# Two quarters of a weight matrix loaded in blocks of 32 partitions

## The chip, the cores and the metric

The kernel runs on one core of one Trainium2 chip. The metric is the device time of one execution in microseconds (us), lower is better. A time of a kernel is the median of several executions. The profile is of one further execution, and its own time is given beside its span, which runs from the first to the last instruction.

## The reference

The computation is a chunked state-space scan over a sequence (4 batches, 8 heads, 768 positions, head width 32, state width 16), followed by a two-layer feed-forward block with a tanh-gelu. Cut to what matters:

```python
for c in range(nc):                       # chunks of the sequence
    cum = np.cumsum(log_a[:, :, sl], axis=-1)
    L = np.exp(cum[..., :, None] - cum[..., None, :]) * causal
    M = np.einsum('bhin,bhjn->bhij', Cc, Bc) * L
    y_intra = np.einsum('bhij,bhjd->bhid', M, xc)
    y_inter = np.einsum('bhin,bhnd->bhid', Cc, state) * np.exp(cum)[..., None]
    y[:, :, sl] = y_intra + y_inter
    state = decay_full * state + sum_j(Bc * xc * decay_from_j)
x = y.transpose(0, 2, 1, 3).reshape(3072, 256)
h = x @ w_in                              # 256 x 2048
g = 0.5 * h * (1 + tanh(c * (h + 0.044715 * h**3)))
out = g @ w_out                           # 2048 x 256
```

`w_in` is 256 x 2048 and `w_out` 2048 x 256, both float32 in memory (2 MB each). The kernel multiplies in bfloat16.

## The kernel before

The 3072 tokens are cut into 24 chunks of 128 (six for each batch), and two neighbouring chunks make a unit `u` of 256 tokens, 12 units in all. A unit passes through two halves. In the scan half TensorE computes `G` (products of C and B), VectorE masks them (`M`), TensorE forms `Y` into the tile yb, and `yev` copies yb into `xm`, the input of the feed-forward half. There `s1.u.i` (eight steps, i = 0 to 7) multiplies `xm` by 256 columns of `w_in` into an accumulator hp, `gelu.u.i` evaluates it into gT on ScalarE, and `s2.u.k.q` multiplies gT by `w_out`; `oev` copies the result out of the accumulator and `store` writes it to memory.

The weights come in quarters. `load_wi(q)` brings 512 columns of `w_in` into a tile `wf` of 128 partitions x 2 x 512 float32: partition d holds the columns of row d and of row 128 + d. Each is 512 KB. `load_wo(q)` brings a quarter of `w_out` into another such tile. `f_wi(q, k, eng)` and `f_wo` (steps `wi.q.k` and `wo.q.k`) then cast one half of such a tile to bfloat16, into `w_in_sb` or `w_out_sb`, each on the engine that the order names. Steps `s1.u.0` and `s1.u.1` use quarter 0 of `w_in`, `s1.u.2` and `s1.u.3` quarter 1, and so on: `s1.0.0` needs `wi.0.0` and `wi.0.1`, `s1.0.2` needs `wi.1.0` and `wi.1.1`, `s1.0.4` quarter 2, `s1.0.6` quarter 3. `s2.0.0.0` needs both halves of `wo.0`.

The order of all steps is written out by hand in the string `ORDERED`: steps are issued in this order, and each engine runs its own ones in that sequence. A suffix names the engine (`:A` ScalarE, `:D` VectorE, `:P` GpSimd, `:S` SyncE's queue), and `~9` stands for small matmuls on zeros (tile wz) that fill time on TensorE. Nearly all loads are issued by SyncE, one after the other: first the inputs of the first batch (`load_bc0`, `load_aq`, `load_x4`, `load_a`), then the weights mixed with later inputs. In the stretch around the change the order of the loads on SyncE is `load_x4`, `load_a.1`, `load_wi.0`, `load_wi.1`, `load_wi.2`, `load_wo.0`, `load_wi.3`, `load_bc1.0`, `load_wo.1`, `load_bc1.1`, `load_wo.2`, `load_wo.3`, and then the inputs of the second batch.

Every load completes on one of eight counters, which the rows of the order call DMAHW0 to DMAHW7. They are taken in rotation over the loads of SyncE and ScalarE together, in the order of the program. A load therefore waits until the load eight places ahead of it has landed, and an instruction that reads a loaded tile waits on the counter of that load. Within the names of the profile, `wf<-in_moe_w_in_dram` is `load_wi`, `x_t<-in_x_dram` of 512 KB is `load_x4`, `a_t<-in_a_dram` is `load_a`, and `bcf` is `load_bc0` and `load_bc1`.

Of the kernel before, what the change touches and what calls it, by code (L numbers as in the profile page):

```python
# [13 lines left out]

XL = 6
WFB = 8

SCR = (2, 3)
ORDERED = """
# [68 lines left out]
def kernel(  # L88
# [10 lines left out]
    nc = tc.nc  # L99
# [21 lines left out]
    ld = ctx.enter_context(tc.tile_pool(name="ld", bufs=2))  # L121
    wfp = ctx.enter_context(tc.tile_pool(name="wfp", bufs=WFB))
    ldx = ctx.enter_context(tc.tile_pool(name="ldx", bufs=XL))
# [21 lines left out]
    XF, X16, WF = {}, {}, {}  # L145
# [39 lines left out]
    wi = moe_w_in.rearrange("(k d) f -> d k f", d=128)  # L185
    wo = moe_w_out.rearrange("(q p k) m -> q p k m", p=128, k=4)

    def load_wi(q):
        WF[("i", q)] = wfp.tile([128, 2, 512], FP32, name="wf")
        nc.sync.dma_start(out=WF[("i", q)], in_=wi[:, :, q * 512:(q + 1) * 512])  # L190

    def load_wo(q):
        WF[("o", q)] = wfp.tile([128, 4, d_model], FP32, name="wf")
# [565 lines left out]
    bl = {(b, i): add("S", load_bc, b, i) for b in range(1, batch) for i in (1, 0)}  # L759
    xl = {u: add("S", load_x, u) for u in range(2, NU)}  # L760
    wl = {(k, q): add("S", f, q) for k, f in (("i", load_wi), ("o", load_wo)) for q in range(4)}

    win = {(q, k): add("P", f_wi, q, k, alt="PAD", deps=[wl[("i", q)]]) for q in range(4) for k in range(2)}
# [86 lines left out]
    for u in range(NU):  # L850
# [23 lines left out]
        for c in cs:  # L874
            if c % CPB == CPB - 1:
                continue
            p, p1 = (None if c % CPB == 0 else pdq if c < R4 else pd), pdq if c < R4 - 1 else pd
# [22 lines left out]
    for u in range(NU):  # L900
        for i in range(NI):
            q = (2 * i + 1) // 4
# [19 lines left out]

    pools = {"hp": 2, "o": 1, "ga": 1, "gb": 1, "yb": 1, "wf": WFB, "xl": XL, "ld": 2, "ob": 6, "st": 4, "sp": 4}
    for w in ORDERED.split():
        if w[0] == "~":
            fill(yb, int(w[1:]))
        else:
            w, _, n = w.partition("+")
# [34 lines left out]
```

## Time and profile before

| | |
|---|---|
| median of 3 executions | 116.68 us (116.48 to 117.45) |
| the profiled execution | 117.7 us, span 116.0 us |
| granted TensorE clock | 1.00 |
| TensorE matmul busy | 110.1 us, 95% of the span |
| VectorE / ScalarE / GpSimd busy | 70.9 / 73.7 / 17.1 us |
| moved by DMA | 15.97 MB, mean 138 GB/s |
| loads of `w_in` | 4 of 512 KB, median 8.0 us from issue to landing |
| loads of `w_out` | 4 of 512 KB, median 8.6 us from issue to landing |

In the rows of the profile PE is TensorE's matmuls, PEld its weight loads, DVE VectorE, ACT ScalarE, POOL GpSimd, SP SyncE, and SPq the DMA queue that SyncE issues to. L316, for instance, is line 316 of the kernel. The line of a copy is that of a helper (`copy`: L314 on ScalarE, L316 on GpSimd, L318 on VectorE), so copies are told apart by the tiles they write. A row of the timeline gives the start in us, the duration, the engine and line, what is written from what, a count, and in brackets the idle time of the engine ahead of it with what ended it. A row on a load (the listing of issues) gives the count, the size and the median time from the start of the issue to the landing.

### The profile page before, as it was taken

Reading aid. Unit: us, or ns where it says so; the run is one execution under the profiler, and the core shown is the slowest. Engines: PE = TensorE matmul, PEld = TensorE weight load, DVE = VectorE, ACT = ScalarE, POOL = GpSimd, SP = SyncE. Lnnn points to the kernel's source line nnn. Section 1 sums busy time; section 2 is a strip of 40 time slices with the busy share of each in tenths; the row PEclk is TensorE's granted clock in tenths of the full one; section 3 lists DMA queues with packets and bytes.
Section 4 is the critical chain, followed back from the end, with each engine's and each line's share of the span. In section 5 each row is a group of like instructions: output and inputs, shape, how many; then the busy total and the mean of one; then the engine's idle time right before and its main releaser. Section 6 shows DMA issues by size and latency. Waiting matters only on the chain.

```text
span 116.0 us, 3378 instructions
## 1 busy us (share of the span) xinstructions
PE 110.1 (95%) x1427; PEld 91.9 (79%) x1427; DVE 70.9 (61%) x139; ACT 73.7 (64%) x142; POOL 17.1 (15%) x35
## 2 busy tenths in 40 slices
PE   6969989999999999999999999999999999999990
PEld 2335568988788897998989889979979898999970
DVE  6589999789979995664967729221968326100000
ACT  3109679996469774766674567776767766776510
POOL 6552556622220220002000000000000000000000
DMA  3999997979979705999869893000014003200222
GB/s 71 235 242 249 403 325 197 359 138 210 221 122 206 156 4 165 178 199 255 164 174 177 206 90 104 0 0 6 0 51 139 0 6 107 74 0 6 90 96 85
DMA packets 43006, 15.97 MB, mean 138 GB/s; under 512 B 36656, under 2 KB 41456, under 8 KB 42992
## 3 DMA queue, kind: packets, MB, share of 16 engines
q1 hardware_dynamic: 42848, 15.68, 57.8%
q8 instruction: 11, 0.18, 0.6%
q10 hardware_dynamic: 144, 0.08, 0.3%
q14 instruction: 3, 0.02, 0.1%
HBM read 11.04 MB, written 3.93 MB: 129 GB/s over the span
## 4 chain that ended last, share of the span: by engine, by line
PE 88%; DVE 2%; ACT 2%; issue 0%
PE hp L709 37%; PE o_ps L727 34%; PE ga L595 3%; PE yb L727 3%; PE yb L659 3%; PE yb L650 3%; PE yb L697 2%; PE hp L628 1%; DVE cz L409 1%; PE hp L425 1%; ACT gT L713 1%; ACT xm L314 1%; DVE pe L387 1%; PE o_ps L563 0%; PE ga L484 0%; DVE s_new L676 0%
## 5 line engine op out<-in xcount | busy, mean ns | idle before, releaser
L713 ACT ACTIVATE gT<-hp 128x512 bf16<-128x512 f32 x96 | 53.9, 596 | 22.0 <-PE hp L709 21.4
L709 PE MATMUL hp<-xm,w_in_sb 128*128 128x256 bf16 x384 | 52.4, 273 | 0.7 <-ACT x L314 0.6
L727 PE MATMUL o_ps<-w_out_sb,gT 128*128 128x256 bf16 x352 | 47.5, 273 | 0.0
L709 PEld LDWEIGHTS <-w_in_sb 128*128 128x128 bf16 x384 | 41.4, 114 | 4.0 <-issue 3.2
L727 PEld LDWEIGHTS <-gT 128*128 128x128 bf16 x384 | 37.0, 98 | 4.2 <-issue 0.2
L605 DVE TENSOR_TENSOR m<-ga,tri 128x1024 bf16<-128x1024 f32 x12 | 14.6, 1216 | 0.3 <-PE gb L595 0.3
L318 DVE COPY o_sb<-o_ps 128x256 f32<-128x256 f32 x13 | 5.5, 423 | 14.6 <-PE o_ps L727 10.9
L605 DVE TENSOR_TENSOR m<-gb,tri 128x1024 bf16<-128x1024 f32 x11 | 13.4, 1214 | 0.0
L697 PE MATMUL yb<-wz 128*128 128x512 bf16 (+3 forms) x26 | 8.1, 459 | 1.1 <-DVE warm L222 1.1
L683 DVE SCALAR_TENSOR_TENSOR sp_new<-s_new,pend,bmask 128x256 bf16<-128x256 f32 x17 | 8.3, 503 | 0.1
L314 ACT ACTIVATE xm<-yb 128x512 bf16<-128x512 f32 x10 | 6.0, 598 | 2.7 <-PE yb L659 2.0
L316 POOL CAST x<-x_t 128x512 bf16<-128x512 f32 x6 | 3.7, 613 | 24.5 <-PE hp L709 9.9
L697 PEld LDWEIGHTS <-wz 128*128 128x128 bf16 x27 | 3.0, 121 | 5.0 <-issue 3.2
L314 ACT ACTIVATE o_sb<-o_ps 128x256 f32<-128x256 f32 x9 | 3.3, 384 | 4.5 <-PE o_ps L727 4.1
L659 PE MATMUL yb<-m,x 128*32 128x128 bf16 x192 | 6.2, 220 | 0.0
L676 DVE SCALAR_TENSOR_TENSOR s_new<-s_new,pend,hp 128x64 f32<-128x64 f32 x13 | 3.6, 279 | 4.1 <-PE hp L628 3.9
L650 PE MATMUL yb<-ce,sp_new 128*32 128x128 bf16 x160 | 5.3, 221 | 0.0
L674 DVE COPY s_new<-hp 128x64 f32<-128x64 f32 x3 | 0.7, 225 | 6.8 <-PE hp L628 6.8
L595 PE MATMUL ga<-ce,bh 32*128 32x256 bf16 x48 | 4.7, 272 | 0.0
L595 PE MATMUL gb<-ce,bh 32*128 32x256 bf16 x48 | 4.7, 273 | 0.0
L316 POOL CAST w_out_sb<-wf 128x512 bf16<-128x512 f32 x6 | 3.9, 672 | 3.7 <-DMA wf<-in_moe_w_out_dram 3.7
L659 PEld LDWEIGHTS <-x 128*32 128x32 bf16 x192 | 3.8, 97 | 0.7 <-issue 0.4
(109 smaller groups left out, 79.6 us busy)
## 6 DMA issues: line engine op xcount, KB each, us to landing
out_dram<-o_sb SPq DMA_DIRECT2D x24, 128.0 KB, 1.8
x_t<-in_x_dram SPq DMA_DIRECT2D x20, 128.0 KB, 3.8
wf<-in_moe_w_in_dram SPq DMA_DIRECT2D x4, 512.0 KB, 8.0
wf<-in_moe_w_out_dram SPq DMA_DIRECT2D x4, 512.0 KB, 8.6
bc_t<-in_B_dram SPq DMA_DIRECT2D x3, 384.0 KB, 4.3
bc_t<-in_C_dram SPq DMA_DIRECT2D x3, 384.0 KB, 4.3
scr<-bc SPq DMA_DIRECT2D x4, 192.0 KB, 2.0
x_t<-in_x_dram SPq DMA_DIRECT2D x1, 512.0 KB, 5.3
```

Of the source, the lines that this page charges most:

```text
L314: nc.scalar.activation(o, i, AF.Copy)
L316: nc.gpsimd.tensor_copy(out=o, in_=i)
L318: nc.vector.tensor_copy(out=o, in_=i)
L595: nc.tensor.matmul(out=gbank(g)[:, 256 * k:256 * k + 256], lhsT=bh_of(2 * u + k)[gs], rhs=ce_of(2 * u + k)[gs], start=True, stop=True, til ...
L605: nc.vector.tensor_tensor(out=m_of(u)[:, 2 * i:2 * i + 2].rearrange("p g k e t -> p (g k e) t"), in0=gx[i].rearrange("p g (k t) -> p (g k) ...
L650: nc.tensor.matmul(out=y4[32 * j:32 * j + 32, k, w], lhsT=sp[:, 32 * h:32 * h + 32], rhs=ce_of(gc)[:, h % 2], start=first(j), stop=False, ...
L659: nc.tensor.matmul(out=y4[32 * j:32 * j + 32, k, w], lhsT=X16[u][:, k, 32 * h:32 * h + 32], rhs=m[:, h // 2, h % 2, :], start=first(j), st ...
L683: nc.vector.scalar_tensor_tensor(out=sp_new.rearrange("p (g d) -> p g d", g=4), in0=(XN[0][:, H * D:H * D + 64] if gc == 0 else state[("s" ...
L697: nc.tensor.matmul(out=t[:, 0:m * 128], lhsT=wz, rhs=w3.to_broadcast([128, m, 128]), start=True, stop=True, skip_group_check=True)
L709: nc.tensor.matmul(out=hp[:, j * T:(j + 1) * T], lhsT=w_in_k[:, w, q, k], rhs=xm[:, w, u * T:(u + 1) * T], start=(w == 0), stop=(w == 1))
L713: nc.scalar.activation(gts[u][:, 2 * i:2 * i + 2], hps.pop((u, i)).rearrange("p (j t) -> p j t", j=2), AF.Gelu_apprx_tanh)
L727: nc.tensor.matmul(out=ops[gc], lhsT=gts[u][:, fi, k * Q:(k + 1) * Q], rhs=w_out_sb[:, fi, :], start=(fi == 0 and (u > 0 or k == 0)), stop ...
```

## The change

`load_wi(0)` and `load_wi(1)` are each issued as four transfers, one for every block of 32 partitions of the tile; `load_wi(2)` and `load_wi(3)` stay one transfer each. The bytes, their places and the order of all steps are the same.

```diff
+WI_PARTS = (4, 4, 1, 1)
...
     def load_wi(q):
         WF[("i", q)] = wfp.tile([128, 2, 512], FP32, name="wf")
-        nc.sync.dma_start(out=WF[("i", q)], in_=wi[:, :, q * 512:(q + 1) * 512])
+        n = 128 // WI_PARTS[q]
+        for p in range(0, 128, n):
+            nc.sync.dma_start(out=WF[("i", q)][p:p + n], in_=wi[p:p + n, :, q * 512:(q + 1) * 512])
```

On SyncE's queue this stands before the change from `load_a.1` to `load_bc1.1`; wf_204, wf_251, wf_258 and wf_433 are the four quarters of `w_in`, and each row ends with the counter that it waits on, the one it will itself complete on:

```order
L162 DMA a_t_99<-in_a_dram 32x384 [waits DMAHW0_49]
L190 DMA wf_204<-in_moe_w_in_dram 128x2x512 [waits DMAHW1_49]
L190 DMA wf_251<-in_moe_w_in_dram 128x2x512 [waits DMAHW2_49]
L190 DMA wf_258<-in_moe_w_in_dram 128x2x512 [waits DMAHW3_49]
L194 DMA wf_303<-in_moe_w_out_dram 128x1024 [waits DMAHW4_49]
L190 DMA wf_433<-in_moe_w_in_dram 128x2x512 [waits DMAHW5_49]
L155 DMA bcf1_101<-in_B_dram 128x8x32 [waits DMAHW6_49]
L194 DMA wf_449<-in_moe_w_out_dram 128x1024 [waits DMAHW7_49]
L155 DMA bcf1_101<-in_C_dram 128x8x32 [waits DMAHW0_49]
```

After the change the same stretch up to `load_bc1.0` reads as follows; lines below the function are three higher, and wf_254, wf_264 and wf_439 are now quarters 1, 2 and 3:

```order
L193 DMA wf_204<-in_moe_w_in_dram 32x2x512 [waits DMAHW1_49]
L193 DMA wf_204<-in_moe_w_in_dram 32x2x512 [waits DMAHW2_49]
L193 DMA wf_204<-in_moe_w_in_dram 32x2x512 [waits DMAHW3_49]
L193 DMA wf_204<-in_moe_w_in_dram 32x2x512 [waits DMAHW4_49]
L193 DMA wf_254<-in_moe_w_in_dram 32x2x512 [waits DMAHW5_49]
L193 DMA wf_254<-in_moe_w_in_dram 32x2x512 [waits DMAHW6_49]
L193 DMA wf_254<-in_moe_w_in_dram 32x2x512 [waits DMAHW7_49]
L193 DMA wf_254<-in_moe_w_in_dram 32x2x512 [waits DMAHW0_49]
L193 DMA wf_264<-in_moe_w_in_dram 128x2x512 [waits DMAHW1_49]
L197 DMA wf_309<-in_moe_w_out_dram 128x1024 [waits DMAHW2_49]
L193 DMA wf_439<-in_moe_w_in_dram 128x2x512 [waits DMAHW3_49]
L156 DMA bcf1_101<-in_B_dram 128x8x32 [waits DMAHW4_49]
```

SyncE issues six transfers more. Quarter 2 used to wait for the load of aq eight places ahead, and now waits for the first part of quarter 0; the loads behind it up to `load_wo.3` wait for parts of quarters 0 and 1 in turn.

GpSimd casts a half of each of the first three quarters; before the change (wf is the quarter's tile, 0, 1 and 2 in this order):

```order
L316 CAST w_in_sb_141<-wf_204 128x512 [waits DMAHW1_49]
L316 CAST w_in_sb_141<-wf_251 128x512 [waits DMAHW2_49]
L316 CAST w_in_sb_141<-wf_258 128x512 [waits DMAHW3_49]
L316 CAST w_in_sb_141<-wf_258 128x512
L316 CAST w_out_sb_142<-wf_303 128x512 [waits DMAHW4_49]
```

And after it:

```order
L319 CAST w_in_sb_141<-wf_204 128x512 [waits DMAHW3_49,DMAHW4_49,DMAHW2_49,DMAHW1_49]
L319 CAST w_in_sb_141<-wf_254 128x512 [waits DMAHW6_49,DMAHW7_49,DMAHW5_49,DMAHW0_49]
L319 CAST w_in_sb_141<-wf_264 128x512 [waits DMAHW1_49]
L319 CAST w_in_sb_141<-wf_264 128x512
L319 CAST w_out_sb_142<-wf_309 128x512 [waits DMAHW2_49]
```

The sequence of the casts is the same. Each cast of quarters 0 and 1 now waits for four counters in place of one, and so do the casts of the same quarters on ScalarE (`wi.0.0`) and VectorE (`wi.1.0`).

## The prediction

> **What bounds the kernel now.** I read the page first. Of the chain that ended last it says:
>
> ```profile
> PE 88%; DVE 2%; ACT 2%; issue 0%
> ```
>
> So the kernel stands on TensorE. Next I cut the span into stages and asked for TensorE alone (columns: stage, its length, TensorE's busy time with its count of matmuls, granted clock, DMA share, GB/s):
>
> ```profile
> 0.00:13.70 13.70, 11.58 (x161) 1.00 0.84 230
> 13.70:16.00 2.30, 1.68 (x16) 1.00 1.12 359
> 16.00:20.00 4.00, 3.90 (x59) 1.00 0.85 230
> 20.00:112.00 92.00, 92.00 (x1195) 1.00 0.54 116
> 112.00:116.00 4.00, 0.93 (x9) 1.00 0.29 98
> ```
>
> From 20 to 112 us TensorE has no idle time at all. The total is thus 92 us plus the drain of 4 us plus whatever it takes to get to the point where TensorE runs through. Only the first 20 us can give or take anything, and there the table of waits lists what TensorE waited for (total, times, longest):
>
> ```profile
> PE yb L697 <- DVE warm L222: 1.1, 1, 1.1
> PE hp L356 <- DVE peq L351: 0.7, 1, 0.7
> PE hp L709 <- ACT x L314: 0.6, 1, 0.6
> PE hp L425 <- DVE cz L409: 0.4, 1, 0.4
> ```
>
> No row names a load, and none names a cast of a weight. The quarters of `w_in` must be on time, but nothing on TensorE waits for them.
>
> **How the loads stand.** SyncE's own timeline shows when each load was issued and how long its issue held SyncE:
>
> ```profile
> 2.86 0.58 SPq L183 DMA_DIRECT2D x_t<-in_x_dram  x1
> 3.49 1.96 SPq L162 DMA_DIRECT2D a_t<-in_a_dram  x1
> 5.50 0.43 SPq L190 DMA_DIRECT2D wf<-in_moe_w_in_dram  x1
> 5.97 0.47 SPq L190 DMA_DIRECT2D wf<-in_moe_w_in_dram  x1
> 6.48 0.47 SPq L190 DMA_DIRECT2D wf<-in_moe_w_in_dram  x1
> 6.99 0.50 SPq L194 DMA_DIRECT2D wf<-in_moe_w_out_dram  x1
> 7.54 0.77 SPq L190 DMA_DIRECT2D wf<-in_moe_w_in_dram  x1
> ...
> 9.07 5.12 SPq L194 DMA_DIRECT2D wf<-in_moe_w_out_dram  x1
> ```
>
> The listing of issues, asked for each of the first seven by itself in the same order, gives the time from the start of the issue to the landing:
>
> ```profile
> x_t<-in_x_dram SPq DMA_DIRECT2D x1, 512.0 KB, 5.3
> a_t<-in_a_dram SPq DMA_DIRECT2D x1, 48.0 KB, 5.2
> wf<-in_moe_w_in_dram SPq DMA_DIRECT2D x1, 512.0 KB, 5.6
> wf<-in_moe_w_in_dram SPq DMA_DIRECT2D x1, 512.0 KB, 7.6
> wf<-in_moe_w_in_dram SPq DMA_DIRECT2D x1, 512.0 KB, 8.4
> wf<-in_moe_w_out_dram SPq DMA_DIRECT2D x1, 512.0 KB, 10.1
> wf<-in_moe_w_in_dram SPq DMA_DIRECT2D x1, 512.0 KB, 10.8
> ```
>
> Adding the two: x4 lands at 8.16, a.1 at 8.69, quarter 0 of `w_in` at 11.1, quarter 1 at 13.57, quarter 2 at 14.88, quarter 0 of `w_out` at 17.09, quarter 3 at 18.34. They land one behind the other in the order of issue, so it is the moving of bytes and not the issuing that sets these times. Against them stand the users, from the timelines of ScalarE, GpSimd, VectorE and TensorE:
>
> ```profile
> 11.90 0.64 ACT L314 ACTIVATE w_in_sb<-wf 128x512 bf16<-128x512 f32 x1
> 12.66 0.60 ACT L314 ACTIVATE xm<-yb 128x512 bf16<-128x512 f32 x1
> ...
> 13.61 0.61 POOL L316 CAST w_in_sb<-wf 128x512 bf16<-128x512 f32 x1 [1.04 <-DMA wf<-in_moe_w_in_dram]
> 14.96 1.49 POOL L316 CAST w_in_sb<-wf 128x512 bf16<-128x512 f32 x2 [0.73 <-DMA wf<-in_moe_w_in_dram]
> 17.16 1.17 POOL L316 CAST w_out_sb<-wf 128x512 bf16<-128x512 f32 x2 [0.71 <-DMA wf<-in_moe_w_out_dram]
> 18.41 0.62 ACT L314 ACTIVATE w_in_sb<-wf 128x512 bf16<-128x512 f32 x1
> ...
> 14.77 0.41 DVE L318 CAST w_in_sb<-wf 128x512 bf16<-128x512 f32 x1
> ...
> 16.00 2.49 PE L709 MATMUL hp<-xm,w_in_sb 128*128 128x256 bf16 x16
> 18.98 0.61 PE L727 MATMUL o_ps<-w_out_sb,gT 128*128 128x256 bf16 x4
> 19.42 0.82 PE L709 MATMUL hp<-xm,w_in_sb 128*128 128x256 bf16 x6
> ```
>
> This gives the lateness that each load can bear before TensorE or a full engine feels it:
> - quarter 0: ScalarE takes it at 11.90, 0.8 us after it landed, and stands idle for 0.12 us between the end of that cast (12.54) and `yev.0` at 12.66. Cover 0.9 us. Behind the cast on ScalarE is queued `yev.0`, for which `s1.0.0` waits.
> - quarter 1: GpSimd was waiting for it and starts at once; VectorE takes its half at 14.77. Cover 1.2 us, and behind it none, since VectorE goes on to the mask of the next unit without a break (its column, the third, below).
> - quarter 2: GpSimd is through at 16.45; `s1.0.4` begins half way through the sixteen matmuls from 16.00, at 17.25. Cover 0.8 us.
> - quarter 0 of `w_out`: GpSimd is through at 18.33, `s2.0.0.0` begins at 18.98. Cover 0.65 us.
> - quarter 3: ScalarE is through at 19.03, `s1.0.6` begins at 19.42. Cover 0.4 us, the smallest.
>
> ```profile
> 13.70:16.00 2.30, 1.68 (x16) 1.18 (x13) 2.30 (x6) 1.28 (x5) 1.57 (x3) 1.00 1.12 359
> ```
>
> If everything from quarter 0 on lands d later, the end moves by d − 0.4 (nothing below 0.4).
>
> **The change part by part.** *Issuing.* Two issues of 0.43 and 0.47 us become eight. From 5.50 at 0.47 each, the first part of quarter 1 goes out at 7.4. The second waits, by the rotation of eight counters, for x4 at 8.16, and with the two after it quarter 1 is issued by 9.6. Quarter 2 now waits for the first part of quarter 0. Quarter 0 moves between 8.69 and 11.1, so its four parts land some 0.6 us apart, at 9.3, 9.9, 10.5 and 11.1, and SyncE's next issues end at about 10.1 (quarter 2), 10.6 (`wo.0`), 11.1 (quarter 3) and 11.8 (`bc1.0`). Queued behind them is `wo.1`, whose issue before the change held SyncE from 9.07 to 14.19. The 2.7 us by which it is now reached later vanish in that hold, unless the hold has another cause than the work ahead in the queue. Does any transfer come too late for its place? Quarter 2 is in the queue by 10.1 and its turn is when quarter 1 is through at 13.57, 3.5 us later; `wo.0` has 4.3 us, quarter 3 6.0 us. A transfer with a free road needs 1.8 us from issue to landing:
>
> ```profile
> out_dram<-o_sb SPq DMA_DIRECT2D x24, 128.0 KB, 1.8
> ```
>
> So the queue does not run dry, and the term is 0. Without that cover it would be the 2.7 us.
>
> *Six more transfers in the queue.* The trace of before has no row of 32 partitions x 2 x 512, so I bound the price of one boundary. From above: a.1, 48 KB on 32 partitions, landed 0.53 us after x4, which it was queued behind. At the 230 GB/s of the first stage its bytes take 0.21 us, so at most 0.3 us is the boundary, 1.8 us for six. From below 0: quarter 2 landed 1.31 us behind quarter 1, and 0.52 MB in 1.31 us is 400 GB/s, which leaves a boundary nothing that shows. A gain is excluded in this term, since the same bytes are moved with six ends more. The row of the neighbouring `w_in` transfers is the nearer one in size and source; I take 0.05 us each, 0.3 us in all, which lies under the cover of 0.4.
>
> *Four waits in place of one* ahead of four casts. Quarter 1 landed at 13.57 and GpSimd began at 13.61, 0.04 us for a wait that ended. Three more are 0.12 us at most. Ahead of ScalarE's cast the idle 0.12 us takes them; VectorE's has no idle time behind it, so I leave up to 0.1 us there. Value: 0 to 0.1.
>
> *What goes away.* GpSimd's idle time of 1.04 us ahead of quarter 1 could shrink if parts landed sooner, but a cast needs all four parts, and next GpSimd waits for quarter 2 anyway.
>
> The sum on the profiled execution is 0 to 0.1 on a span of 116.0, with 1.7 us around it (117.7 in all). The median of the three runs, 116.68, is 1.0 lower than that execution, and the change is added to the median: 116.7.
>
> **A rule against it.** The listing of stages has the GB/s while `w_in` moves:
>
> ```profile
> 8.70:11.60 2.90, 2.86 (x62) 1.50 (x60) 2.73 (x8) 2.82 (x8) 0.70 (x2) 1.00 0.97 249
> 11.60:14.50 2.90, 2.69 (x80) 1.55 (x78) 2.87 (x8) 1.95 (x6) 1.58 (x3) 1.00 1.03 403
> ```
>
> Quarters 0 and 1, 1.05 MB, took from 8.69 to 13.57, 4.88 us or 215 GB/s, though 403 is reached right behind. The Trainium skill, "SBUF — State Buffer", section "Door 1: The DMA port swizzle", says that a transfer into partitions 0 to 31 reaches 8 of 16 ports, 189 GB/s at 1 MiB against 328 over 128 partitions, and a later section of that page that two transfers to different halves still serialize; by its 189 the two quarters would take an estimated 5.5 us, 0.7 more than now, and the end 0.3 us later, 117.0. No run before shows such a transfer alone.
>
> **The rivals.** *Slower: parts of 32 partitions move at half the rate.* Every part writes a quarter of the partitions, and the four follow each other in one queue. Half of 403 is 202 GB/s, at which 1.05 MB takes 5.2 us. If that rate replaces what holds the two quarters at 215 now, they are 0.3 late and the cover takes it: 116.7. If it comes on top (at 403 the bytes would take 2.6 us, so 2.28 us of the present 4.88 are stalls, and 5.2 + 2.28 = 7.5) they are 2.6 us late, and quarter 3 makes that 2.2 us: 118.9. The middle, 1.1 us, is 117.8. It decides from d = 1.6 on. For it speaks that nothing in the profile shows such parts at full rate; against it that the two quarters already move at nearly that pace. *Slower: the boundary at its upper price*, 1.8 − 0.4 = 1.4: 118.1. Against it speaks quarter 2 behind quarter 1. *Faster: the loads land earlier*, because the later quarters are issued later and share the engines less. TensorE's idle time from 13.70 to 20 is 0.62 + 0.10; were all of it due to loads, the time would be 116.0. Its waits name no load, which speaks against even that.
>
> **How the numbers follow.** The measurement can tell about 1%, 1.2 us, from no change. Forecast (all under cover, 116.7): 0.70. Half rate, 0.17, of which 0.09 is above 1.2 us. Boundary, 0.08, of which 0.02 is. Earlier, 0.05, within 1% by its bound. For effects outside these mechanisms I put 0.03 on either side, out of the forecast's share. So slower 0.14, faster 0.03, same 0.83. The range reaches down to the earlier loads with a little for the spread of the median, 116.0, and up to the boundary's price, 118.1; beyond it lie the upper part of the half rate and the unforeseen.
>
> **What would show it.** Right: SyncE shows eight issues of about 0.45 us with a short hold at the sixth, `wo.1` ends its issue near 14.2 again, quarter 1's casts start within 0.5 us of before, TensorE's waits name no load and it stays without idle time from 20 us. Half rate: the first slice of the two has clearly under 249 GB/s, and ScalarE or TensorE waits for a load of `w_in`. Boundary: landings of parts more than 0.25 us apart beyond their bytes. Wrong altogether: a time that moves by over 1% while the casts of quarter 3 start where they did.

## The result, and the profile after

The changed kernel takes 117.42 us (median of 20 executions, 116.84 to 118.81), the kernel before, on the same chip, 116.91 us (20 executions, 116.01 to 118.42). The ratio is 1.0052, with a 95% interval of 1.0033 to 1.0071: about 0.6 us slower, less than 1%, but more than nothing. The profiled execution of the changed kernel took 117.91 us with a span of 115.9.

Each execution gives its time and its span, so the difference can be split. The median span is 115.45 us after the change (18 undisturbed executions) and 115.0 to 115.05 before it (22, 34 and 32 executions beside the experiments): 0.4 us more. What lies outside the span, time less span of the same execution, is 1.95 us (1.89 to 2.01) after and 1.73 us (1.67 to 1.79) before: 0.22 us more. Two different things have to be found.

The answers of the profile to the places that the prediction named. The same stages for TensorE alone (columns as before: length, busy time, clock, DMA share, GB/s):

```profile
0.00:13.70 13.70, 11.60 (x162) 1.00 0.89 218
13.70:16.00 2.30, 1.81 (x15) 1.00 1.04 368
16.00:20.00 4.00, 3.91 (x59) 1.00 0.98 262
20.00:112.00 92.00, 91.86 (x1193) 1.00 0.52 116
```

From 20 us on TensorE still runs through, but for 0.14 us at 27.7. Its waits in the changed kernel:

```profile
PE yb L700 <- DVE warm L225: 1.1, 1, 1.1
PE hp L359 <- DVE peq L354: 0.7, 1, 0.7
PE hp L712 <- ACT x L317: 0.5, 1, 0.5
PE hp L428 <- DVE cz L412: 0.4, 1, 0.4
```

They are the same four, and none is a load. This is the trap of the case: the profiled execution of before (span 116.0) was one of the longer ones, about 1 us over its kernel's median, and the two profiles look alike. A difference of 0.4 us doesn't show when one execution is laid beside one other.

The loads did what the prediction worked out from the order. SyncE's timeline after the change, each issue by itself (start, time that it held SyncE):

```profile
4.87 0.42 SPq L193 DMA_DIRECT2D wf<-in_moe_w_in_dram  x1
...
6.28 0.42 SPq L193 DMA_DIRECT2D wf<-in_moe_w_in_dram  x1
6.75 0.42 SPq L193 DMA_DIRECT2D wf<-in_moe_w_in_dram  x1
...
8.62 0.31 SPq L193 DMA_DIRECT2D wf<-in_moe_w_in_dram  x1
8.97 0.43 SPq L193 DMA_DIRECT2D wf<-in_moe_w_in_dram  x1
```

These are parts 1 and 4 of quarter 0 and parts 1, 3 and 4 of quarter 1. The listing of issues gives 4.3 us to landing for parts 1 and 2 of quarter 0, and then:

```profile
wf<-in_moe_w_in_dram SPq DMA_DIRECT2D x1, 128.0 KB, 4.5
wf<-in_moe_w_in_dram SPq DMA_DIRECT2D x1, 128.0 KB, 4.5
wf<-in_moe_w_in_dram SPq DMA_DIRECT2D x1, 128.0 KB, 4.6
wf<-in_moe_w_in_dram SPq DMA_DIRECT2D x1, 128.0 KB, 3.8
wf<-in_moe_w_in_dram SPq DMA_DIRECT2D x1, 128.0 KB, 4.1
```

which are part 4 of quarter 0 and the four of quarter 1. Quarter 0 is complete at 6.28 + 4.5 = 10.8 us, quarter 1 at 8.97 + 4.1 = 13.1; before it was 11.1 and 13.57. (Landings below that are given to 0.01 us come from the completion events of the trace, of which the listing prints tenths.) So both quarters landed a little earlier, not later.

What that did is seen on GpSimd and VectorE. GpSimd's timeline after the change:

```profile
11.76 0.60 POOL L319 CAST w_in_sb<-wf 128x512 bf16<-128x512 f32 x1
13.09 0.61 POOL L319 CAST w_in_sb<-wf 128x512 bf16<-128x512 f32 x1 [0.72 <-DMA wf<-in_moe_w_in_dram]
```

and VectorE's in the same execution:

```profile
11.84 1.33 DVE L334 TENSOR_TENSOR_SCAN r_t<-ac,ends 64x384 f32<-64x384 f32 x1
13.10 0.24 DVE L679 SCALAR_TENSOR_TENSOR s_new<-s_new,pendq,hp 128x64 f32<-128x64 f32 x1
13.27 0.44 DVE L388 TENSOR_TENSOR pe<-ac,r_t 64x3 f32<-64x3 f32 x1
13.75 0.17 DVE L390 TENSOR_TENSOR pe<-pe,m 64x24 f32<-64x24 f32 x1
13.85 0.27 DVE L679 SCALAR_TENSOR_TENSOR s_new<-s_new,pendq,hp 128x64 f32<-128x64 f32 x1
```

The cast of quarter 0 starts 0.08 us ahead of the scan, the cast of quarter 1 runs beside the small `pe` of 64x3. To see that this matters one needs an execution in which they don't meet. The experiment with spare loads (below) leaves the first 60 us as they are in the kernel before; its GpSimd:

```profile
11.96 0.88 POOL L322 CAST w_in_sb<-wf 128x512 bf16<-128x512 f32 x1 [0.51 <-DMA wf<-in_moe_w_in_dram]
13.41 0.75 POOL L322 CAST w_in_sb<-wf 128x512 bf16<-128x512 f32 x1 [0.58 <-DMA wf<-in_moe_w_in_dram]
```

and its VectorE:

```profile
11.48 0.94 DVE L337 TENSOR_TENSOR_SCAN r_t<-ac,ends 64x384 f32<-64x384 f32 x1
12.35 0.25 DVE L682 SCALAR_TENSOR_TENSOR s_new<-s_new,pendq,hp 128x64 f32<-128x64 f32 x1
12.52 0.33 DVE L391 TENSOR_TENSOR pe<-ac,r_t 64x3 f32<-64x3 f32 x1
12.88 0.17 DVE L393 TENSOR_TENSOR pe<-pe,m 64x24 f32<-64x24 f32 x1
13.01 0.28 DVE L682 SCALAR_TENSOR_TENSOR s_new<-s_new,pendq,hp 128x64 f32<-128x64 f32 x1
```

Here the cast came 0.48 us after the scan had begun, the scan took 0.94 us instead of 1.33, and it is the cast that stretched, from 0.60 to 0.88 us. From the start of the scan to the second `s_new` it is 13.01 − 11.48 = 1.53 us without the collision and 13.85 − 11.84 = 2.01 us with it. This stretch lies on the path: the second `s_new` releases ScalarE's copy `x`, and that releases `s1.0.1` on TensorE, which is the third wait in the list above. The kernel before can collide as well. In its profiled execution quarter 0 landed at 11.1, its cast began 0.08 us ahead of the scan, and VectorE shows the same picture, with the second cast under the other `pe`:

```profile
12.04 1.32 DVE L331 TENSOR_TENSOR_SCAN r_t<-ac,ends 64x384 f32<-64x384 f32 x1
...
13.65 0.60 DVE L387 TENSOR_TENSOR pe<-pe,m 64x24 f32<-64x24 f32 x1
14.18 0.27 DVE L676 SCALAR_TENSOR_TENSOR s_new<-s_new,pendq,hp 128x64 f32<-128x64 f32 x1
```

The Trainium skill, "SBUF — State Buffer", section "🔬 SBUF: two separate sides", says that VectorE and GpSimd share one pair of ports as an exclusive lock: an operation of VectorE with two SBUF inputs and one of GpSimd that reads SBUF exclude each other, and the one that starts first keeps the ports for its whole length. The traces agree: the first to start keeps its own time (cast 0.60, or scan 0.94), the other takes longer (scan 1.33; cast 0.88 here, and 1.23 in the kernel with ticks on VectorE, where it began 0.11 us behind the scan).

### The profile page after: what moved, and what is told of

The parts are those of the page before. It is cut to its first block, busy times and chain, and to the rows that moved or that the text cites. A ratio compares the mean times of both kernels' runs of the same rounds, so it can differ in the third digit from the quotient of the medians.

```text
span 115.9 us, 3392 instructions
## 1 busy us (share of the span) xinstructions
PE 109.9 (95%) x1427; PEld 91.8 (79%) x1427; DVE 70.5 (61%) x139; ACT 73.7 (64%) x142; POOL 17.4 (15%) x35
## 4 chain that ended last, share of the span: by engine, by line
PE 84%; DVE 5%; ACT 2%; issue 1%; DVEq 0%
PE hp L712 35%; PE o_ps L730 32%; PE ga L598 3%; PE yb L730 3%; PE yb L662 3%; PE yb L653 2%; PE yb L700 2%; DVE m L608 1%; DVE bc L478 1%; PE hp L631 1%; DVE pt L385 1%; DVE cz L412 1%; PE hp L428 1%; ACT gT L716 1%; ACT xm L317 1%
```

## The experiments

The first question was which property of the change counts: the blocks of 32 partitions, the number of transfers, or the time of landing. Every kernel was timed against the kernel before on the same chip. Spans and times outside the span are medians.

**Four parts of every fourth partition in place of blocks.**

```diff
-        n = 128 // WI_PARTS[q]
-        for p in range(0, 128, n):
-            nc.sync.dma_start(out=WF[("i", q)][p:p + n], in_=wi[p:p + n, :, q * 512:(q + 1) * 512])
+        n = WI_PARTS[q]
+        for p in range(n):
+            nc.sync.dma_start(out=WF[("i", q)][p:128:n], in_=wi[p:128:n, :, q * 512:(q + 1) * 512])
```

> The change with another choice of partitions: each of the four transfers of quarters 0 and 1 takes every fourth partition (0, 4, 8, ... and so on) in place of 32 neighbouring ones. Number of transfers, their bytes, their rows of 2 KB and all waits are those of the changed kernel. Theory 'half rate' (parts of 32 neighbouring partitions move slowly, and that makes the 0.5 us): the stage 11 to 13 us is back near 400 GB/s, quarter 3 lands earlier, and the time is back at the kernel before, ratio 0.999 to 1.001. Theory 'six more transfers' (each has a price of its own, wherever it falls): ratio 1.004 to 1.007 as with the change.

Measured: ratio 1.0055 (1.0034 to 1.0076), span 115.5, outside 1.90. The same price, so it doesn't hang on the block of neighbouring partitions alone. The parts land faster here (quarter 0 at 9.56 us), but each issue holds SyncE 0.60 us in place of 0.43. The price is not made up the same way, either: in this kernel's profiled execution quarter 2 landed only at 15.80 us, and `s1.0.4` began 0.05 us behind its cast, 0.56 us later after `s1.0.3` than in the changed kernel.

**Only quarter 0 in parts.**

```diff
-WI_PARTS = (4, 4, 1, 1)
+WI_PARTS = (4, 1, 1, 1)
```

> Only quarter 0 is loaded in four parts, quarter 1 in one. Three more transfers than before, not six. 'Six more transfers': half of the change, ratio 1.0025. 'Half rate': quarter 0 lands when it did (it moved at 210 to 250 GB/s before), so ratio 1.000 to 1.001; the loss of the change would sit in quarter 1.

Measured: ratio 1.0063 (1.0035 to 1.0092), span 115.6, outside 1.96. Half of the change costs as much as all of it, so the price is not one per transfer.

**All four quarters in parts.**

```diff
-WI_PARTS = (4, 4, 1, 1)
+WI_PARTS = (4, 4, 4, 4)
```

> All four quarters of w_in in four parts each, twelve more transfers. 'Six more transfers': twice the change, ratio 1.010. 'Half rate': quarters 2 and 3 moved at some 400 GB/s before, at half of that they land 1.3 us and 2.6 us later, so 2 us on the time, ratio 1.017, and ScalarE waits for quarter 3 by 2 us.

Measured: ratio 1.0196 (1.0165 to 1.0228), 2.3 us on 116.7, span 117.55, outside 1.73. Here the pace of the parts shows. In the completion events the first twelve parts land within 6.40 us, 0.58 us for each 0.131 MB or 225 GB/s, right through the stretch in which the kernel before reached 403 GB/s; SyncE could have issued them 0.47 us apart, so the moving sets this pace. Its profiled execution, with a span of 118.8, is 1.2 us over the kernel's median, in part because it began late (`s1.0.0` at 14.47 us, in the changed kernel at 13.49); from `s1.0.0` to the end it took 104.29 us against 102.44. The windows of this kernel, all engines (the last number is GB/s):

```profile
11.60:14.50 2.90, 2.90 (x111) 1.53 (x85) 2.87 (x8) 2.14 (x6) 1.72 (x3) 1.00 0.93 238
14.50:17.40 2.90, 2.57 (x22) 1.92 (x19) 2.90 (x7) 2.12 (x6) 0.65 (x2) 1.00 0.97 267
```

and now casts of `w_in` stand among TensorE's waits:

```profile
PE hp L712 <- ACT w_in_sb L317: 0.9, 1, 0.9
...
PE hp L712 <- POOL w_in_sb L319: 0.5, 1, 0.5
```

The slow pace of the parts is thus real, and it costs as soon as quarters 2 and 3 are moved that way. Whether it comes from the 32 partitions, from the size of 128 KB or from a price for each transfer's end (at 403 GB/s the bytes of a part take 0.33 us, which would leave 0.25 of the 0.58) was not separated. The first three parts of every fourth partition, of the same size and queued behind other loads, landed 0.30 and 0.31 us apart, which speaks for the partitions; the later ones came out of SyncE only every 0.64 us, too slowly to tell.

**The kernel before with six loads more,** 16 KB each on 32 partitions, in the middle of the run where nothing waits for them.

```diff
+    def f_spare(i):
+        p = 32 * (i % 4)
+        nc.sync.dma_start(out=spare[p:p + 32], in_=wi[p:p + 32, :, 0:64])
```

> The kernel before, with six loads of 32 partitions x 2 x 64 (16 KB each) into a tile that nobody reads, issued by SyncE near 72 us, where it has nothing else to do and TensorE runs through. 'Six more transfers' with a price outside the start (ahead of or behind the span, or anywhere on the way): ratio 1.002 to 1.006, by the part of the 0.5 us that is not tied to the place. 'Half rate', or any cause at the place of the weights: 1.000, within 0.001.

Measured: ratio 1.0002 (0.9979 to 1.0026), span 115.05, outside 1.73. No price of the transfers shows in the time (the interval leaves room for 0.3 us), and none outside the span. A small one is there all the same, at the end of the span. ScalarE's last copy, before and after the change:

```profile
112.96 0.38 ACT L314 ACTIVATE o_sb<-o_ps 128x256 f32<-128x256 f32 x1 [1.31 <-PE o_ps L727]
```

```profile
112.78 0.38 ACT L317 ACTIVATE o_sb<-o_ps 128x256 f32<-128x256 f32 x1 [1.31 <-PE o_ps L730]
```

From its start to the end of the span (115.96 and 115.93) it is 3.00 us before and 3.15 after. The last store lands 2.1 us after that start in both. Behind the landing SyncE goes through waits for the remaining counters one by one, 0.06 to 0.07 us each, two of them before the change and four after it, and what closes the program follows. With the spare loads it is four waits and 3.12 us. In the other kernels with quarters 0 and 1 in parts it is four waits and 3.13 to 3.15 us, with only one of them in parts three waits and 3.10 to 3.11, and in all kernels with the loads of before two waits and 2.99 to 3.00. (With all four quarters in parts it is four waits and 3.53; more on this below.) The likely reason is that further loads move the rotation on, so that the last store completes on another counter; no run varies that alone. So about 0.15 us of the 0.4 in the span lie here.

**Only quarter 1 in parts.**

```diff
-WI_PARTS = (4, 4, 1, 1)
+WI_PARTS = (1, 4, 1, 1)
```

> Only quarter 1 is loaded in four parts; quarter 0 goes back to one transfer. Theory 'early quarter 0' (split, quarter 0 of w_in lands about 1 us earlier; GpSimd then begins to cast it ahead of VectorE's scan at line 331 instead of behind its start, the scan takes 1.33 us in place of 0.94, and s1.0.1 and all behind it come later): quarter 0 lands late again, the scan is back at 0.94 us in most executions, ratio 0.999 to 1.001. Rival 'any part of the split costs' (queue, waits, rate of the parts): about half of the change, ratio 1.0025 or more.

Measured: ratio 1.0053 (1.0025 to 1.0081), span 115.3, outside 2.00. In its profiled execution quarter 0, one transfer here, landed at 10.00 us, 1.47 us ahead of the scan, and the collision was there again. So the theory's expectation failed here; why quarter 0 landed so early with its own transfer unchanged is not shown.

**The kernel before with the collision forced:** GpSimd's cast of quarter 0 reads a tile that is there earlier, and the loads stay as they are. This kernel thereby leaves half of quarter 0 of `w_in` out of the products.

```diff
-        copy(eng, w_in_sb[:, k, q * 512:(q + 1) * 512], WF[("i", q)][:, k])
+        src = x4_t[:, 0:4].rearrange("p h t -> p (h t)") if (q, k) == (0, 1) else WF[("i", q)][:, k]
+        copy(eng, w_in_sb[:, k, q * 512:(q + 1) * 512], src)
```

> The kernel before, all loads unchanged, but GpSimd's cast of its half of quarter 0 reads a tile that landed long before (x4_t, the same shape), so it never waits for w_in; half of quarter 0 of the weights is thereby not the right one. 'Early quarter 0': the cast always begins right behind the mask step of GpSimd, ahead of the scan, the scan takes 1.33 us, and without any change of a load the loss of the change is there, ratio 1.003 to 1.005. Rival (the loads themselves cost): 1.000 or a little below.

Measured: ratio 1.0031 (1.0009 to 1.0053), span 115.35, outside 1.73. VectorE's timeline:

```profile
11.99 1.33 DVE L332 TENSOR_TENSOR_SCAN r_t<-ac,ends 64x384 f32<-64x384 f32 x1
...
13.97 0.27 DVE L677 SCALAR_TENSOR_TENSOR s_new<-s_new,pendq,hp 128x64 f32<-128x64 f32 x1
```

1.98 us from scan to second `s_new`: the collision alone, without one transfer more, costs about 0.3 us of span (0.1 to 0.6 by the interval of the ratio), and nothing outside.

**A hold of 0.3 us ahead of GpSimd's first cast,** in the changed kernel and in the kernel before. The same edit in both:

```diff
+    def f_hold():
+        nc.gpsimd.memset(spare, 0.0)
...
-... G.1 M.1.0 M.1.1 wi.0.1:P s1.0.0 S.1.1
+... G.1 M.1.0 M.1.1 hold wi.0.1:P s1.0.0 S.1.1
```

> The changed kernel with a memset of some 0.3 us on GpSimd (a tile that nobody reads) ahead of its cast of quarter 0, so that the scan on VectorE begins first. 'Early quarter 0': the scan takes 0.94 us, the span goes back to that of the kernel before or below, ratio 0.998 to 1.002 (the upper end if the 0.2 us outside the span stay). Rival: 1.005 as before, or more.

> The kernel before with the same memset on GpSimd ahead of the same cast. 'Early quarter 0': the few executions in which quarter 0 was early enough to collide are gone, so the same or a little faster, ratio 0.997 to 1.000, and the scan takes 0.94 us. Rival: 1.000 to 1.002, since an instruction was added.

Measured: in the changed kernel ratio 1.0054 (1.0029 to 1.0078), span 115.2, outside 2.07; in the kernel before ratio 1.0012 (0.998 to 1.0043), span 114.85, outside 1.85. In the first the scan was back at 0.94 us, but the cast that now came behind it pushed the next one into `pe` (0.58 us), so one collision took the place of the other. And one small instruction on GpSimd made both kernels 0.12 us longer outside their span.

**Two holds, ahead of the casts of quarters 0 and 1,** in both kernels.

```diff
-... M.1.1 wi.0.1:P s1.0.0 S.1.1
+... M.1.1 hold.0 wi.0.1:P s1.0.0 S.1.1
-... load_bc1.0 wi.1.1:P gelu.0.1
+... load_bc1.0 hold.1 wi.1.1:P gelu.0.1
```

> Theory (a GpSimd cast that runs into VectorE's stretch from the scan to the second s_new costs about 0.45 us in the span): with the cast of quarter 0 and the cast of quarter 1 both moved back by a short GpSimd memset, neither meets the stretch; the second s_new starts 1.5 to 1.6 us after the scan and the median span goes back from 115.45 to 115.05 or less. The time outside the span stays at 1.9 to 2.1, so the ratio to before comes to 1.001 to 1.004. Rival (the span grew for another reason, the order of landing or the six transfers): the distance may shrink but the span stays at 115.4 and the ratio at 1.005.

> The kernel before with the same two memsets. Theory: it collides in some of its executions only, so its median span falls slightly, 114.8 to 115.05, its outside grows to about 1.85 as with one memset, ratio 0.998 to 1.002. Rival (the memsets themselves move the span): span 115.3 or more, ratio 1.003 or more.

Measured: in the changed kernel ratio 1.0061 (1.0031 to 1.009), span 115.35, outside 2.20; in the kernel before ratio 1.0026 (0.9997 to 1.0055), span 114.95, outside 2.04. The distance from scan to second `s_new` came back to 1.52 us in the changed kernel, as expected, yet its span did not fall to 115.05. This speaks against the collision as the only cause in the span. About 0.14 us of what is left lie behind the last store's landing (3.14 us from the last copy). VectorE's timeline has no stretched operation in that distance:

```profile
11.34 0.94 DVE L339 TENSOR_TENSOR_SCAN r_t<-ac,ends 64x384 f32<-64x384 f32 x1
...
12.86 0.28 DVE L684 SCALAR_TENSOR_TENSOR s_new<-s_new,pendq,hp 128x64 f32<-128x64 f32 x1
```

Right behind it an `sp_new` took 0.79 us in place of 0.47, beside the cast of quarter 1, but TensorE lost nothing by that. GpSimd's timeline shows the next limit:

```profile
17.75 0.61 POOL L319 CAST w_in_sb<-wf 128x512 bf16<-128x512 f32 x1 [1.03 <-DMA wf<-in_moe_w_in_dram]
```

and TensorE's what it does:

```profile
17.68 0.61 PE L735 MATMUL o_ps<-w_out_sb,gT 128*128 128x256 bf16 x4
18.41 1.08 PE L717 MATMUL hp<-xm,w_in_sb 128*128 128x256 bf16 x8
```

`s1.0.6` begins 0.05 us after this cast of quarter 3 ends, and 0.73 us after the matmuls ahead of it; with spare loads those two starts are 17.82 and 18.27, 0.45 us apart. TensorE came early and found quarter 3 missing: 0.28 us in this execution.

**Six tiny instructions more on GpSimd, or on VectorE,** in the kernel before, in the middle of the run.

```diff
+    def f_tick(i):
+        nc.gpsimd.memset(spare, 0.0)        # nc.vector in the other kernel
+    for i in range(6):
+        add("P", f_tick, i)
```

> The kernel before with six tiny memsets on GpSimd in the middle of the run, off every path. Theory (the time outside the span depends on how much is in GpSimd's program): span 115.05, outside 1.85 to 2.1, ratio 1.001 to 1.003. Rival (it depends on something else that the change does): outside 1.73, ratio 1.000.

> The same six tiny memsets on VectorE. Theory (only GpSimd's program counts): outside 1.73, span 115.05, ratio 1.000. Rival (any engine's program counts): outside 1.85 to 2.1, ratio 1.001 to 1.003. VectorE is 61% busy there, so the span should not move under either.

Measured: on GpSimd ratio 1.005 (1.0015 to 1.0085), span 115.1, outside 2.21 (2.15 to 2.23); on VectorE ratio 1.0015 (0.9985 to 1.0046), span 115.15, outside 1.73. So the time outside the span goes with the number of instructions in GpSimd's program, and not with VectorE's or SyncE's.

How many does the change add there? The head of the page, of before and of after, counts them:

```profile
span 116.0 us, 3378 instructions
```

```profile
span 115.9 us, 3392 instructions
```

Fourteen more. Six are the issues; the other eight belong to the four casts that now wait for four counters in place of one, two more instructions for each. Two of these casts are GpSimd's, so its program grows by four, and the events of the trace count 62 there before and 66 after. (The Trainium skill, "Perfetto Trace Analysis", section "Identifying Dependency Chains", says that instructions that wait on several engines may have semaphore instructions put ahead of them. Here the waits are for loads, and the count fits.) The kernels by GpSimd's count, with the time outside the span:

| GpSimd instructions more than before | kernels | outside the span, us |
|---|---|---|
| 0 | before, spare loads, forced collision, VectorE ticks | 1.73 |
| 1 | before with one hold | 1.85 |
| 2 | only quarter 0, only quarter 1, before with two holds | 1.96, 2.00, 2.04 |
| 4 | every fourth partition, the change | 1.90, 1.95 |
| 5 | the change with one hold | 2.07 |
| 6 | the change with two holds, GpSimd ticks | 2.20, 2.21 |
| 8 | all four quarters | 1.73 |

Kernels with the same count agree within 0.08 us, whatever else differs in them; from this agreement, and from no run of its own, comes that a wait counts there like a memset. The rise is about 0.13 us for one instruction, with a fall somewhere between two and four and another between six and eight. What happens there is not known: it lies outside the span, and no view shows it. The last fall may be less than it looks: in the profiled execution of the kernel with all four quarters in parts, 0.42 us in place of 0.08 pass inside the span between two of GpSimd's last instructions, so part of the time may have moved there.

## Why the prediction was right or wrong

The time stayed within 1% and in the range, as forecast; "everything under cover" was nevertheless not what happened, since 0.6 us was lost. That the number held is in part luck: the prices that the sum had at nothing, the collision, the end of the run and the time outside the span, happen to be small.

*Issuing, 0.* Right. Eight issues of 0.31 to 0.43 us, with a hold ahead of the seventh part (at 8.62, just behind x4's landing at 8.60) and not of the sixth. The issue of `wo.1` held SyncE for 1.44 us in place of 5.12 and ended at 12.85, not near 14.2; the issues behind it were held in turn, and `wo.1` landed at 20.03 us against 20.02. The lateness of the issues vanished as the prediction had it.

*Six boundaries, 0.3 us under cover.* Not seen at the weights. The parts of quarter 0 land 0.51 to 0.57 us apart, which is 0.131 MB at 230 to 257 GB/s; at the 230 GB/s that the prediction reckoned with, this leaves no room for a boundary, and as a loss of 1.4 us the rival at 118.1 falls. Whether the pace itself holds a price for each transfer is not separated (see the kernel with all four quarters in parts). Further transfers do have a price at a place that the sum doesn't look at: 0.15 us behind the landing of the last store, where nothing covers it.

*The half rate.* The slow pace is real, and the variant to which the rival gave the price of nothing is the one that came. From part to part quarter 0 moved at 246 GB/s and quarter 1 at 221; but the two had moved at 215 before, so there was nothing to lose there. The place where the full rate was used lies behind them, and when the parts reach into it the price is 2.3 us (in the profiled execution 0.5 of it at the end of the run, 3.53 us against 3.00). The rule of the Trainium skill, "SBUF — State Buffer", section "Door 1: The DMA port swizzle", on partitions 0 to 31 fits the pace in kind, with 221 to 246 where that page has 189 at 1 MiB; by the prediction's estimate from it the quarters would have landed later and cost 0.3 us, and they did not land later.

*What goes away.* This step failed. It valued GpSimd's shorter wait at nothing, "a cast needs all four parts, and next GpSimd waits for quarter 2 anyway". It asked what an earlier cast could gain on GpSimd, and not what else the cast excludes while it runs. An earlier cast meets VectorE's scan, and that costs 0.48 us between the scan and the second `s_new` (2.01 against 1.53), of which the forced collision leaves 0.3 us in the median span. TensorE runs the same 1427 matmuls in the same order in every kernel here, so the loss can be read from their starts: from `s1.0.0` to `s1.0.1` it takes 0.66 or 0.67 us in the six profiled executions without a stretched operation between the scan and the second `s_new`, and 0.95 to 1.38 in the eight with one. The rival "loads land earlier" was right in that they did and had the wrong sign.

How often the collision comes is set by the landing of quarter 0. In the seven profiled executions whose loads up to there are those of the kernel before, it landed 0.5 to 2.6 us ahead of the scan four times (before, forced collision, one hold, two holds) and 0.06 to 0.42 us behind it three times (spare loads, both kinds of ticks). In the seven with quarter 0, quarter 1 or more in parts it landed 0.7 to 2.0 us ahead every time. With no hold in between, a cast then met this stretch of VectorE every time. So the kernel before meets it in a good part of its own executions, and the change adds it to the others.

*The covers.* They were read right from the profile, but from an execution with a collision in it, in which TensorE reached `s1.0.1` 0.6 us later than it does undisturbed (14.91 − 12.04 = 2.87 us from the start of the scan, against 13.76 − 11.48 = 2.28 with spare loads). A wait on the path is a cover for everything behind it. In undisturbed executions quarter 3 has less than the 0.4 us given: in the profiled execution with six ticks on GpSimd, whose front is that of the kernel before, it landed late and TensorE's waits name it (0.4 us, `w_in_sb` on ScalarE, as a fourth wait), and with two holds the changed kernel lost 0.28 us to it. Removing the collision from the changed kernel therefore gave little. Nor is TensorE as steady behind 20 us as its busy time says: the hundred matmuls from about 27 to 33 us take 6.23 us in eight of the fourteen profiled executions and 6.3 to 6.6 in six, the profiled ones of before and after among them.

*Four waits in place of one, 0 to 0.1 us.* Mis-sized, and in the wrong place. As idle time on the engines they cost nothing that shows; as instructions on GpSimd they cost 0.22 us outside the span, which the sum had carried over as a constant 1.7.

What is settled: 0.22 us of the loss lies outside the span and goes with GpSimd's instruction count; of the 0.4 us in the span about 0.15 lie behind the landing of the last store, and the collision can make 0.3. What is open: how much of the 0.4 is the collision in the mean over executions and how much is quarter 3's landing, since the kernel with both casts held back kept its 115.35, of which the end of the run explains about 0.14. That quarter 3 lands later on the mean because of the parts' pace is argued, not shown. It landed at 17.70 to 18.52 us in the four profiled executions with quarters 0 and 1 in parts, and at 16.78 to 18.46, with 17.21 as the median, in the seven with the loads of before, which leans that way; but this spread at the same front is wider than the effect, and with only one of the two quarters in parts it landed at 17.25 and 17.48 for the same price. No version that beats the kernel before was found; the one with the lowest span, 114.85 with one hold, gives 0.12 of its 0.2 us back outside the span and can't be told from the kernel before.

## What to carry to other kernels

An earlier landing is not a gain by itself: ask which engine it sets free, and what that engine's work excludes when it starts there, GpSimd's casts beside VectorE's two-input operations above all. Read covers from an execution near the median span, since a stall on the path looks like cover for every load behind it. And for differences of half a per cent compare spans and times outside the span separately, over many executions, before looking for a cause in a single trace.

## What the runs showed of the hardware

- A GpSimd cast of 128x512 float32 and a VectorE operation with two SBUF inputs block each other: scan 0.94 to 1.33 us, a `pe` of 64x24 0.17 to 0.60 us, or the cast 0.60 to 0.88 us and more when it is the second to start.
- Behind the landing of the last store SyncE passes its remaining waits at 0.06 to 0.07 us each; with four of them in place of two the span ends 0.12 to 0.15 us later.
- An instruction that waits for four counters is accompanied by two further instructions on its engine.
- One instruction more in GpSimd's program can lengthen the time outside the span by about 0.13 us, up to 0.48 us for six; six on VectorE, or six loads on SyncE, leave it at 1.73 us.
- Issuing a load on every fourth partition holds SyncE 0.60 us, one on 32 neighbouring partitions 0.43 us.
